# Joining float64 words with one shift-and-or in an attention and expert-layer kernel on one core

## The chip, the cores and the metric

The kernel runs on one core of a Trainium2 chip. The core has a matrix engine (TensorE, PE in the profile, its weight loads PEld), a vector engine (DVE), an activation engine (ACT), a general engine (POOL, nearly unused here) and a queue that issues DMAs (SP). Each engine runs its own list of instructions in order, and they wait for one another by semaphores. The metric is the device time of one execution in microseconds. Before the change its median over three runs is 596.85 us (596.62 to 597.36).

## The reference

Causal attention over 4 batches of 12 heads, 448 positions and 64 columns per head, then two matrix products with an ELU between them. The weights `moe_w_in` and `moe_w_out` are float64.

```python
def _attn_ref(q, k, v):
    scores = scale * np.matmul(q, k.transpose(0, 1, 3, 2))
    scores = np.where(mask, -1000000000.0, scores)
    scores = scores - np.max(scores, axis=-1, keepdims=True)
    attn = np.exp(scores)
    attn = attn / (np.sum(attn, axis=-1, keepdims=True) + 1e-09)
    return np.matmul(attn, v).astype(np.float32)

def _moe_ref(x, w_in, w_out):          # x: 1792 x 768, w_in: 768 x 2048, w_out: 2048 x 768
    h = x @ w_in
    g = np.where(h > 0.0, h, alpha * (np.exp(np.minimum(h, 0.0)) - 1.0))
    return (g @ w_out).astype(np.float32)
```

## The kernel before

**Attention.** Two heads share the 128 partitions. For each pair of heads PE forms the scores (sc, line 535), DVE adds the mask and takes the row minimum of the negated scores (line 440), ACT takes the exponential with the row sums (line 444), PE transposes (tr, line 566), a copy brings the transpose to SBUF (at, on ACT at line 570 or on DVE at line 571), and PE multiplies with the values (av, line 585). The six head pairs of batch 0 come first of all, two at a time (`first_two`); the other batches are spread between the matmuls of the expert layer.

**The expert layer.** A float32 product is done as three products of a high and a low part (hp and op, lines 786 to 788). The split into the parts is `hi_lo` (lines 741 to 748): the high part is a copy to a shorter type, on ACT (line 744) or DVE (line 745), the low part a subtraction on DVE (line 747). `in_two` (line 735) does that for a weight tile of 128 x 768 (whl), `split_row` (line 862) for a row of activations (ph, pl). For batches 2 and 3, and for the second product of all, seven products of combined blocks stand in place of eight (`mixed`, `mixed_h`, `mixed_o`), for which DVE adds and subtracts blocks.

**Float64 weights.** The chip gets each weight as two 32-bit words. `convert` (line 697) makes float32 of a tile of 16 x 768 columns (w_in, one for each of 16 blocks) or 512 columns (w_out, 24 tiles). It clamps the high word as a float (DVE, line 705), rescales it on ACT so that its exponent comes right (line 709), shifts the bits left by three (DVE, line 710), takes the top three bits of the low word (ACT, line 713) and adds them to the shifted word (DVE, line 716, a custom operation on halves of 16 bits in the profile). The result is split for the matmuls and stored to DRAM for later use.

**The order of work.** The kernel first writes all of its instructions as a list of works (`plan.add`), each with one or two ways to be done (an engine, a cost and a function), its buffers and a due time from the order of PE's matmuls. `draft` then goes through them like a scheduler: the engine that can start soonest takes, of the works that can start by then, that with the earliest wanted time. The wanted time is the due time less an entry of the table `SOONER`, by the number of the work; a positive entry draws the work forward. A work with two ways stays with the first (ACT) unless the second (DVE) would be done at least `LEAST` = 0.8 us sooner:

```python
                    if way:
                        if w.want > s + self.SOON:
                            continue
                        ...
                        if max(t, free.get(e0, 0.0)) + before + c0 < s + cost + self.LEAST:
                            continue
```

The order that comes out is the order of each engine's instruction list, SP's DMAs included.

Of the kernel before, what the change touches and what calls it, by code (L numbers as in the profile page):

```python
# [11 lines left out]
U32 = mybir.dt.uint32  # L12
# [96 lines left out]
class Plan:  # L109
# [21 lines left out]
    def add(self, ways, reads=(), writes=(), due=None, size=0.0, hold=(), after=None):  # L131
# [24 lines left out]
        return w  # L156

    SOONER = {
# [50 lines left out]
    }  # L209

    def rank(self):
# [17 lines left out]
    def draft(self, shift):  # L229
# [17 lines left out]
        while len(order) < len(self.works):  # L247
            starts = {}
            for w, t in ready.items():
# [19 lines left out]
                for way, (eng, cost, _, port) in enumerate(w.ways):  # L269
                    s = max(t, free.get(eng, 0.0))  # L270
                    if w.size and w.want > s + self.FAR:
                        s = max(s, moved - self.QUEUE)
                    if port:
                        s = max([s] + [f for e, f in ported.items() if e != eng])
                    if way:
                        if w.want > s + self.SOON:
                            continue
                        e0, c0 = w.ways[0][:2]
                        before = sum(
                            o.ways[0][1] for o, to in ready.items()  # L280
                            if to <= s and o.ways[0][0] == e0 and o.want < w.want and o is not w
                        )
                        if max(t, free.get(e0, 0.0)) + before + c0 < s + cost + self.LEAST:
                            continue
                    starts.setdefault(eng, []).append((s, w.want, w.n, way, w))
# [51 lines left out]
def attention_moe_kernel(ctx, tc, qk, v, w_in, w_out, out):  # L337
# [62 lines left out]
    def act(n, fn, more=0.05):  # L400
        return ("ACT", more + 0.84e-3 * n, fn, False)

    def dve(n, fn, rate=1.05e-3, more=0.067, port=False):
        return ("DVE", more + rate * n, fn, port)
# [294 lines left out]
    def convert(key):  # L699
# [7 lines left out]
        ), 0.55e-3, 0.06, True), [(r, 1)], [w])  # L707

        plan.add(act(size, lambda: nc.scalar.activation(wf(), wf(), AF.Prelu, scale=REBIAS, alpha=2.0 ** 32), 0.09), [], [w])  # L709
        plan.add(dve(size, lambda: nc.vector.tensor_scalar(  # L710
            wf().bitcast(U32), wf().bitcast(U32), 3, None, op0=ALU.logical_shift_left
        ), 0.55e-3, 0.06, True), [], [w])
        plan.add(act(size, lambda: nc.scalar.activation(
            low().bitcast(I32), low(), AF.Copy, scale=2.0 ** -29
        ), 0.16), [], [(r, 0)])
        plan.add(dve(size, lambda: nc.vector.tensor_tensor(  # L716
            out=wf().bitcast(I32), in0=wf().bitcast(I32), in1=low().bitcast(I32), op=ALU.add
        ), 1.05e-3, 0.07, port=True), [(r, 0)], [w])
        if key[0] == "i":
            done(r)  # L720
            home, src = kin[key[1]], wf
# [470 lines left out]
```

## Time and profile before

| what | us |
|---|---|
| median of three runs | 596.85 |
| profiled execution | 597.11 |
| its span, first to last instruction | 595.3 |
| PE busy (share of the span) | 585.1 (98%) |
| PEld busy | 518.4 (87%) |
| DVE busy | 516.5 (87%) |
| ACT busy | 434.9 (73%) |
| POOL busy | 1.5 (0%) |

The profile is of one execution. Busy time is the time in which an engine has at least one instruction running; matmuls overlap, so that a busy PE may still run slower than it can. A line such as L786 is a line of the kernel; the names are those of the program's tiles, written `out<-in`. "Idle before" is the time in which an engine had nothing to run just before a group of instructions, with the engine that ended it. The granted clock is the share of full speed that the chip gave to TensorE.

### The profile page before, as it was taken

Reading aid. Unit: us, or ns where it says so; the run is one execution under the profiler, and the core shown is the slowest. Engines: PE = TensorE matmul, PEld = TensorE weight load, DVE = VectorE, ACT = ScalarE, POOL = GpSimd, SP = SyncE. Lnnn points to the kernel's source line nnn. Section 1 sums busy time; section 2 is a strip of 40 time slices with the busy share of each in tenths; the row PEclk is TensorE's granted clock in tenths of the full one; section 3 lists DMA queues with packets and bytes.
Section 4 is the critical chain, followed back from the end, with each engine's and each line's share of the span. In section 5 each row is a group of like instructions: output and inputs, shape, how many; then the busy total and the mean of one; then the engine's idle time right before and its main releaser. Section 6 shows DMA issues by size and latency. Waiting matters only on the chain.

```text
span 595.3 us, 11387 instructions
## 1 busy us (share of the span) xinstructions
PE 585.1 (98%) x4010; PEld 518.4 (87%) x4010; DVE 516.5 (87%) x1236; ACT 434.9 (73%) x996; POOL 1.5 (0%) x12
## 2 busy tenths in 40 slices
PE   7999999999999999999999999999999999999998
PEld 4767798889899898898888988999999999999997
DVE  5798999998989989999998899869888999998532
ACT  6999999897988889988786593455555768575310
POOL 0000000000000000000000000000000000000000
PEclk9989999999999999999999999999999999999999
DMA  8987976488689999796556579987854115344112
GB/s 245 407 281 241 297 247 188 161 269 278 177 270 347 329 313 339 238 299 204 157 134 197 164 231 334 332 276 232 261 165 132 54 55 184 96 137 133 52 40 74
DMA packets 81976, 127.58 MB, mean 214 GB/s; under 512 B 9472, under 2 KB 58112, under 8 KB 81920
## 3 DMA queue, kind: packets, MB, share of 16 engines
q1 hardware_dynamic: 81920, 126.87, 67.1%
q8 instruction: 31, 0.51, 0.3%
q14 instruction: 25, 0.20, 0.1%
HBM read 94.63 MB, written 32.21 MB: 213 GB/s over the span
## 4 chain that ended last, share of the span: by engine, by line
PE 91%; ACT 5%; DVE 2%; DMA 0%; issue 0%; SPq 0%; DVEq 0%
PE op L786 12%; PE hp L786 12%; PE op L787 12%; PE op L788 11%; PE hp L788 11%; PE hp L787 11%; PE av L585 7%; PE sc L535 7%; PE tr L566 6%; ACT a L444 3%; PE hp L809 2%; ACT at L570 1%; ACT w L709 1%; DVE a L440 1%; DMA k<-in_qk 0%; DVE w L716 0%
## 5 line engine op out<-in xcount | busy, mean ns | idle before, releaser
L786 PE MATMUL op<-ph,whl 128*128 128x448 f32 (+1 forms) x338 | 125.7, 372 | 0.0
L787 PE MATMUL op<-pl,whl 128*128 128x448 f32 (+1 forms) x338 | 123.4, 365 | 0.1
L788 PE MATMUL op<-ph,whl 128*128 128x448 f32 (+1 forms) x338 | 123.3, 365 | 0.0
L744 ACT ACTIVATE whl<-w 128x768 fp32r<-128x768 f32 x101 | 83.9, 840 | 53.6 <-PE op L788 36.5
L444 ACT ACTIVATE a<-a,nm 112x336 f32<-112x336 f32 (+3 forms) x192 | 99.8, 529 | 25.2 <-DVE nm L440 24.8
L747 DVE TENSOR_TENSOR whl<-w,whl 128x768 fp32r<-128x768 f32 x111 | 104.4, 951 | 3.2 <-ACT whl L744 2.6
L440 DVE CUSTOM_DVE_ANT_0 a<-sc,mask 112x448 f32<-112x448 f32 (+3 forms) x192 | 76.0, 444 | 12.3 <-PE sc L535 12.3
L786 PE MATMUL hp<-xh,whl 128*128 128x448 f32 x180 | 69.9, 388 | 0.0
L786 PEld LDWEIGHTS op<-ph,whl 128*128 128x128 f32 x338 | 63.5, 188 | 6.5 <-issue 0.6
L787 PEld LDWEIGHTS op<-pl,whl 128*128 128x128 f32 x338 | 63.5, 188 | 5.3 <-DVE pl L747 0.5
L788 PEld LDWEIGHTS op<-ph,whl 128*128 128x128 f32 x338 | 63.5, 188 | 5.2
L788 PE MATMUL hp<-xh,whl 128*128 128x448 f32 x180 | 65.9, 366 | 1.1 <-DVE whl L747 1.1
L787 PE MATMUL hp<-xl,whl 128*128 128x448 f32 x180 | 65.8, 366 | 0.0
L787 PE MATMUL hp<-pl,whl 128*128 128x448 f32 x168 | 61.4, 365 | 0.0
L786 PE MATMUL hp<-ph,whl 128*128 128x448 f32 x168 | 61.4, 365 | 0.0
L788 PE MATMUL hp<-ph,whl 128*128 128x448 f32 x168 | 61.4, 365 | 0.0
L566 PEld LDWEIGHTS tr<-ident,a 112*112 112x112 f32 x480 | 49.4, 133 | 10.2 <-ACT a L444 2.8
L570 ACT ACTIVATE at<-tr 112x448 f32<-112x448 f32 x116 | 56.5, 542 | 2.1 <-PE tr L566 2.1
L566 PE MATMUL tr<-ident,a 112*112 112x112 f32 x480 | 56.4, 260 | 1.6 <-ACT a L444 1.0
L585 PEld LDWEIGHTS av<-at,v 112*64 112x64 f32 x960 | 47.3, 139 | 8.9 <-issue 3.7
L585 PE MATMUL av<-at,v 112*64 112x112 f32 x960 | 52.9, 265 | 0.5 <-ACT at L570 0.4
L882 ACT ACTIVATE m<-hp 128x448 f32<-128x448 f32 x56 | 29.9, 541 | 25.1 <-PE hp L788 15.7
(94 smaller groups left out, 951.4 us busy)
## 6 DMA issues: line engine op xcount, KB each, us to landing
w<-kin SPq DMA_DIRECT2D x41, 384.0 KB, 5.0
w<-in_w_in SPq DMA_DIRECT2D x16, 768.0 KB, 7.8
w<-in_w_out SPq DMA_DIRECT2D x24, 512.0 KB, 6.0
w<-sout SPq DMA_DIRECT2D x32, 384.0 KB, 3.6
w<-kout SPq DMA_DIRECT2D x24, 384.0 KB, 3.4
kin<-w SPq DMA_DIRECT2D x16, 384.0 KB, 6.0
sout<-w SPq DMA_DIRECT2D x12, 512.0 KB, 5.9
sin<-w SPq DMA_DIRECT2D x16, 384.0 KB, 4.4
```

What stands on the lines that cost most here:

```text
L440: plan.add(dve(n, lambda: nc.vector.tensor_tensor_reduce(out=a()[:, c], in0=sc()[:, c], in1=mask[:, S - n:], op0=ALU.add, op1=ALU.min, sca ...
L444: plan.add(act(n, lambda: nc.scalar.activation(a()[:, c], a()[:, c], AF.Exp, bias=nm()[:, x:x + 1], scale=-1.0, accum_out=su()[:, x:x + 1] ...
L535: nc.tensor.matmul(sc[half]()[:, lo:lo + n], q(d, x, i), k(d, y, n), start=j == 0, stop=j == len(split) - 1,)
L566: nc.tensor.transpose(tr()[:, chunk(x)], group["a"][half]()[:, chunk(x)], ident)
L570: act(w, lambda: nc.scalar.activation(at()[:, :w], tr()[:, :w], AF.Copy)),
L585: nc.tensor.matmul(av()[half_of(half), chunk(i)], u["v"]()[:, half, c], at()[:, chunk(x)], start=c == 0, stop=c == i,)
L744: act(n, lambda: nc.scalar.activation(h(), x(), AF.Copy), 0.09),
L747: sub = lambda eng: lambda: eng.tensor_tensor(out=l(), in0=x(), in1=f32(h()), op=ALU.subtract)
L786: nc.tensor.matmul(acc(), wh(k), xh(), start=first, stop=False, skip_group_check=more)
L787: nc.tensor.matmul(acc(), wh(k), xl(), start=False, stop=False, skip_group_check=more)
L788: nc.tensor.matmul(acc(), wl(k), xh(), start=False, stop=last, skip_group_check=more)
L882: plan.add(act(S, lambda: nc.scalar.activation(m(), h(), AF.Relu, scale=-1.0), 0.14), [h], [m])
```

## The change

Three things change. In `convert` the shift of the high part and the extraction of the low bits become two ways of one work: ACT takes the low bits with a scale and a bias that make it round down, or DVE shifts the high part. A single scalar_tensor_tensor on DVE then shifts the other word and joins the two with a bitwise or. The fixed shift and the integer addition go. The table `SOONER` is replaced by another (484 entries in place of 394). A new table `WAY` fixes the way of 70 works (0 is the first way, ACT; 1 is the second, DVE), and `draft` follows it without the comparison above.

```diff
     SOONER = {
-        12: -55.9, 54: -74.4, 55: -11.4, 87: -3.7, 88: 96.4, 91: -8.2, 93: -22.7, 105: 26.2, 131: -16.6,
...
+        12: -19.4, 27: 20.6, 28: 91.9, 34: 2.8, 43: 60.4, 44: -72.9, 54: 38.6, 55: 79.7, 67: -11.3, 73:
...
+    WAY = {
+        44: 0, 95: 1, 228: 1, 275: 1, 278: 0, 283: 1, 288: 1, 297: 1, 446: 1, 449: 0, 462: 1, 534: 0,
+        728: 0, 801: 1, 810: 1, 817: 1, 819: 1, 844: 0, 901: 1, 1006: 0, 1042: 1, 1066: 1, 1187: 1,
+        1216: 0, 1218: 1, 1304: 0, 1317: 0, 1342: 0, 1380: 1, 1382: 1, 1426: 1, 1667: 1, 1679: 1, 1693:
+        1, 1818: 1, 1822: 1, 1854: 1, 1867: 1, 1896: 0, 1930: 1, 1934: 1, 2000: 1, 2001: 1, 2056: 1,
+        2058: 1, 2106: 1, 2206: 1, 2262: 1, 2444: 0, 2455: 1, 2557: 1, 2591: 1, 2608: 1, 2621: 1, 2648:
+        1, 2685: 1, 2689: 1, 2710: 1, 2779: 1, 2804: 1, 2806: 0, 2846: 1, 2848: 1, 2850: 1, 2861: 1,
+        2876: 1, 2904: 1, 2908: 1, 2917: 1, 2979: 1,
     }
...
-                    if way:
+                    if self.WAY.get(w.n, way) != way:
+                        continue
+                    if way and w.n not in self.WAY:
                         if w.want > s + self.SOON:
                             continue
...
-        plan.add(dve(size, lambda: nc.vector.tensor_scalar(
-            wf().bitcast(U32), wf().bitcast(U32), 3, None, op0=ALU.logical_shift_left
-        ), 0.55e-3, 0.06, True), [], [w])
-        plan.add(act(size, lambda: nc.scalar.activation(
-            low().bitcast(I32), low(), AF.Copy, scale=2.0 ** -29
-        ), 0.16), [], [(r, 0)])
-        plan.add(dve(size, lambda: nc.vector.tensor_tensor(
-            out=wf().bitcast(I32), in0=wf().bitcast(I32), in1=low().bitcast(I32), op=ALU.add
-        ), 1.05e-3, 0.07, port=True), [(r, 0)], [w])
+        bits, shifted = (lambda: wf().bitcast(U32)), []
+        plan.add([
+            act(size, lambda: nc.scalar.activation(
+                low().bitcast(I32), low(), AF.Copy, scale=2.0 ** -29 * (1.0 - 2.0 ** -20), bias=-0.4999
+            ), 0.16),
+            dve(size, lambda: (shifted.append(1), nc.vector.tensor_scalar(
+                bits(), bits(), 3, None, op0=ALU.logical_shift_left
+            )), 0.55e-3, 0.06, True),
+        ], [(r, 0)], [(r, 0), w])
+
+        def join():
+            x, by, how, y = (low(), 29, ALU.logical_shift_right, bits()) if shifted else (bits(), 3, ALU.logical_shift_left, low())
+            nc.vector.scalar_tensor_tensor(out=bits(), in0=x, scalar=by, in1=y, op0=how, op1=ALU.bitwise_or)
+        plan.add(dve(size, join, 1.05e-3, 0.07, port=True), [(r, 0)], [w])
```

## Rows read from the trace of the kernel before

**Rows 1.** The page: share of the chain that ended last, by engine.
```profile
PE 91%; ACT 5%; DVE 2%; DMA 0%; issue 0%; SPq 0%; DVEq 0%
```

**Rows 2.** PE's waits; last row, its weight loads' from 10 to 46: us, times, longest.
```profile
PE hp L788 <- DVE whl L747: 1.1, 1, 1.1
PE tr L566 <- ACT a L444: 1.0, 1, 1.0
PE tr L566 <- DVE xf L609: 0.5, 1, 0.5
PE av L585 <- ACT at L570: 0.4, 1, 0.4
...
PEld av L585 <- DVE w L710: 1.3, 1, 1.3
```

**Rows 3.** DVE in order of time, 218 to 241: start us, us, instruction [idle before].
```profile
221.98 0.43 DVE L710 TENSOR_SCALAR w<-w 128x512 uint32<-128x512 uint32 x1 [0.86 <-ACT w L709]
...
234.44 0.95 DVE L747 TENSOR_TENSOR whl<-w,whl 128x768 fp32r<-128x768 f32 x1
```

**Rows 4.** Busy time by stretch: length, PE, PEld, DVE, ACT, POOL, granted clock, DMA.
```profile
15.00:31.00 16.00, 13.98 (x166) 10.86 (x164) 12.00 (x41) 16.00 (x49) 0.00 (x0) 1.00 1.03 402
31.90:35.30 3.40, 3.40 (x26) 2.09 (x28) 3.23 (x10) 3.27 (x13) 0.00 (x0) 0.51 1.04 289
60.00:210.00 150.00, 150.00 (x1193) 131.91 (x1191) 139.45 (x388) 135.75 (x331) 0.00 (x0) 1.00 0.81 258
210.00:240.00 30.00, 28.73 (x203) 25.22 (x200) 28.38 (x82) 27.48 (x70) 0.00 (x0) 1.00 0.98 325
480.00:540.00 60.00, 60.00 (x298) 55.60 (x297) 59.57 (x101) 41.77 (x76) 0.00 (x0) 1.00 0.38 115
```

**Rows 5.** PE in order of time, at 30 to 48 and 228 to 242 us.
```profile
30.56 1.25 PE L566 MATMUL tr<-ident,a 112*112 112x112 f32 x8 [1.02 <-ACT a L444]
...
33.35 3.09 PE L585 MATMUL av<-at,v 112*64 112x112 f32 x40
...
45.06 2.14 PE L585 MATMUL av<-at,v 112*64 112x112 f32 x40
...
235.46 0.47 PE L788 MATMUL hp<-xh,whl 128*128 128x448 f32 x1 [1.14 <-DVE whl L747]
```

**Rows 6.** Groups by line and shape, conversion: busy us, mean ns of one | idle before.
```profile
L713 ACT ACTIVATE w<-w 128x512 int32<-128x512 uint32 x24 | 16.1, 679 | 0.0
L716 DVE CUSTOM_DVE_ANT_0 w<-w,w 128x1536 uint16<-128x1536 uint16 x16 | 15.3, 955 | 0.5
L713 ACT ACTIVATE w<-w 128x768 int32<-128x768 uint32 x16 | 14.6, 948 | 0.0
L710 DVE TENSOR_SCALAR w<-w 128x512 uint32<-128x512 uint32 x24 | 10.2, 424 | 5.8 <-ACT w L709 5.6
L710 DVE TENSOR_SCALAR w<-w 128x768 uint32<-128x768 uint32 x16 | 8.9, 554 | 0.9 <-ACT w L709 0.9
```

**Rows 7.** Groups by line and shape: the nearest forms, and two-way works on DVE.
```profile
L747 DVE TENSOR_TENSOR whl<-w,whl 128x768 fp32r<-128x768 f32 x111 | 104.4, 951 | 3.2 <-ACT whl L744 2.6
L747 DVE TENSOR_TENSOR pl<-G,ph 128x448 fp32r<-128x448 f32 x64 | 37.8, 619 | 0.2
...
L745 DVE CAST whl<-w 128x768 fp32r<-128x768 f32 x10 | 5.6, 556 | 0.1
L884 DVE SCALAR_TENSOR_TENSOR u<-m,u 128x448 f32<-128x448 f32 x8 | 4.9, 618 | 0.1
L571 DVE COPY at<-tr 112x448 f32<-112x448 f32 x4 | 2.5, 621 | 0.8 <-PE tr L566 0.8
L745 DVE CAST ph<-s 128x448 fp32r<-128x448 f32 x2 | 0.8, 387 | 0.0
```

**Rows 8.** Chain that ended last, in order of time, 26 to 32: start us, us.
```profile
27.43 0.84 ACT w L713
28.27 0.85 ACT at L570 x2
```

More of the change, by code (lines that the diff above doesn't have):

```diff
@@ L158 @@
     SOONER = {
[50 rows of a table removed]
[61 rows of a table added]
+    }
+    WAY = {
[7 rows of a table added]
     }
```

109 rows, old and new, of the table SOONER are left out of this document.

## The prediction, made before the changed kernel ran

> **What bounds the kernel now.** The chain that ended last comes first. Of it, 91% is PE's, 5% ACT's and 2% DVE's [rows 1]. So an edit that touches only DVE and ACT can give no more than PE's lost time, wherever the cause of a loss is DVE or ACT. The list of PE's waits is the next view, since it says where that is. Beside the wait for the first load, which stays, it has four: 1.0, 0.5 and 0.4 us in the attention work at the start, and one of 1.1 us for a weight split by DVE (line 747), which DVE began at 234.44 us [rows 2, 3]. The table of stretches then shows how full each engine was where PE lost. From 15 to 31 us ACT is busy for all of its 16.00 us and PE for 13.98. In 210:240 PE has 28.73 of 30.00, DVE 28.38 and ACT 27.48. From 60 to 210 us, and from 480 to 540 us, PE is never idle, though DVE is nearly full (139.45 of 150, 59.57 of 60) [rows 4]. One loss more shows only in PE's granted clock: 0.51 from 31.9 to 35.3 us, so close to the lower of its levels (1.2 GHz of 2.4). Just before it PE had sat idle for 1.02 us until 30.56 us. The same 40 products of the values (av) took 3.09 us in that stretch and 2.14 us at 45 us [rows 4, 5]. So 0.95 us is lost on these alone, and at most 3.4 x 0.49 = 1.7 us in all; I take 1.5, since little else lies in the stretch and nearly all of it is PE's work.
>
> What DVE or ACT could give back is then about 1.1 us at 234, some 1.9 us of waits at the start (1.0 + 0.5 + 0.4), and 1.5 us of clock: 4.5 us, 0.8%. Nothing else is in reach of this change, unless tighter switching between kinds of matmuls brings some tenths.
>
> **The change, part by part.** *The conversion.* Before, each of 40 float64 tiles (16 of 768 columns, 24 of 512) costs five instructions: a clamp on DVE, a rescale on ACT, a shift on DVE (L710), the low bits on ACT (L713), and a join on DVE (L716). After, the shift and the low bits are alternatives, so each tile has four. If ACT takes the low bits, DVE loses the shift: 16 x 0.554 + 24 x 0.424 = 8.9 + 10.2 = 19.1 us, were it so for all 40. If DVE shifts, ACT loses the low bits: 16 x 0.948 + 24 x 0.679 = 15.2 + 16.3 = 31.5 us by duration, 30.7 us by busy time [rows 6]. Back to back, DVE's instructions overlap by about 0.1 us. Nothing of this is PE's, so the gain is only what reaches the places above.
>
> *The new join.* One scalar_tensor_tensor on 32-bit words replaces a custom operation on 16-bit halves, which takes 955 ns for 768 words. The form with two bitwise operations does not occur before. Nearest rows: a scalar_tensor_tensor with both inputs in SBUF (u<-m,u) takes 618 ns for 448 columns, and a tensor_tensor on the same size 619; a tensor_tensor on 768 takes 951 [rows 6, 7]. On the tensor_tensor's line, (951 - 619) / 320 = 1.04 ns per column and 154 ns on top, 512 words take 686 ns. I take 951 and 686: no change. Below, it could run like the one-input shift (554 and 424), which would save 16 x 0.40 + 24 x 0.27 = 12.8 us of DVE. Above, twice the slope gives 1.75 and 1.22 us, or 16 x 0.80 + 24 x 0.53 = 25.5 us more. The Trainium skill speaks for that upper end: "Vector Engine (DVE) Microarchitecture Reference", section "Points that are easy to get wrong", says that a scalar_tensor_tensor whose two sources lie in SBUF and are not bf16 runs at half throughput. The trace disagrees for floats with its 618 ns against 619; for words no row shows it.
>
> The low bits get a bias as an immediate and lose a rounding. An activation with a scale and no bias is in the trace already; I take the same 948 and 679 ns. The low bits or the shift now also wait for the rescale. On ACT that costs nothing where the rescale is ahead in its queue anyway. Behind a shift that waits stands the rest of DVE's queue, as behind L710 before. No DMA is added and none dropped; the store of a converted tile follows its join as before.
>
> *Which engine.* I counted the works in the order in which the code adds them, less one for each conversion already passed. All 70 numbers of the new table then fall on works with two ways. They are 18 weight splits (15 to DVE), 26 row splits (22 to DVE), 8 query/key splits (6), 9 copies of transposes (8), 7 conversions (4), one other copy (to DVE) and one other split. The rest go by the old rule, which leaves a work on ACT unless DVE is sooner by 0.8 us. DVE so gets at least 15 x 0.556 + 22 x 0.387 + 8 x 0.621 = 21.8 us, against 10 x 0.556 + 6 x 0.387 + 4 x 0.621 = 10.4 us of the same kinds before [rows 7]: 11.4 us more. With some 30 conversions left to ACT it loses 30/40 x 19.1 = 14.3 us. So DVE's total falls by about 3 us (by 8 if ACT takes the low bits of all 40, and it rises by 11 if of none). The larger relief is ACT's: 10/40 x 31.5 = 8 us of low bits, and the moved splits and copies besides.
>
> *At 234 us.* PE waits for the split that DVE began at 234.44 us. In the 13 us ahead of it DVE ran three shifts of 0.43 us, the first at 221.98 us [rows 3]. Without them the split comes up to 1.29 us sooner, less what the first shift's own wait for ACT (0.86 us) keeps. The stall is 1.14 us [rows 5]. I take -1.1 (bounds 0, if these tiles are shifted by DVE, and -1.3, which is PE's whole idle time in 210:240 [rows 4]).
>
> *At the start.* In the chain of waits ACT stands without a break there. One low-bits extraction (0.84 us) stands in it ahead of the exponentials for which PE waits until 30.56 us [rows 5, 8]. DVE shifts that tile anyway, so on DVE's side it is free. One copy of a transpose that the table gives to DVE takes another 0.43 us (two take 0.85) from ACT [rows 8]. Together -1.27, of which PE can use up to the 1.02 us that it waited. I take -0.9 (bounds 0 and -1.9, all three waits). If the cover goes, that is if DVE, which has 4 of 16 us free there [rows 4], runs late with the copy, the 0.62 us [rows 7] is PE's wait.
>
> *Behind it.* The weight loads of the products that begin at 33.35 us (on the row of PE's loads) wait 1.3 us on DVE, in a queue that a shift (L710) holds up [rows 2, 5]. Without the shift, 0.554 us less the overlap, -0.45 (bounds 0 and -1.3).
>
> *The clock and the order.* The fall to 0.51 stays in my sum: PE still has waits ahead of it. The table of moved works is new throughout (394 entries before, 484 after), and its effect on PE I take as 0, with bounds from the small waits: -1 to +2.8 (below).
>
> Sum: -1.1 - 0.9 - 0.45 = -2.45 us. The profiled execution took 597.11 us, which is 1.8 us around its span of 595.3, and stands 0.26 us over the median of 596.85. From the median: 594.4 us.
>
> **The rivals.** *The clock does not fall at the start.* With the waits of 0.5 and 1.0 us gone, PE may stay at 2.4 GHz: -1.5 more, 592.9 us. For it: the fall comes right behind such a wait. Against: ACT is full from 15 to 31 us, and PE can lack work there without such a wait.
>
> *No change.* PE had only one wait behind 31 us; the new order brings one or two like it elsewhere (1.1 us each) and eats the gains: 596.3 us. For it: DVE and ACT are still both over 90% in 60:210 [rows 4], so any work that is late meets a queue.
>
> *Slower: the works fixed on DVE in 480:540.* By their due times eight of these are there: three weight splits and five row splits, 3 x 0.556 + 5 x 0.387 = 3.6 us, against the two row splits on DVE before (ph<-s, 0.8 us) [rows 7]. DVE has 0.43 us free in 60 [rows 4], so it falls back by 2.4 us by 540. PE pays as soon as its lead over DVE is less than that. Against: PE never waited in that stretch, and behind 540 us DVE waits for PE. Price: 2.4 us with none of the start's gains and half of the gain at 234: 596.85 + 2.4 - 0.55 = 598.7 us.
>
> *The join at half speed.* DVE then has 25.5 us more and 14.3 less, or +11.2, nearly all between 31 and 260 us, where it has 10.55 us free in 60:210. Some 4 us reach PE: 600.9 us. It is the mechanism that the page's rule gives, and the floats' row speaks against it.
>
> **How the numbers follow.** Forecast 0.40 (594.4), clock stays up 0.20 (592.9), no change 0.22 (596.3), slower by DVE 0.14 (598.7), join at half speed 0.04. What can be told from no change is 0.2%, 1.2 us: 595.65 to 598.05. The forecast ends within that in one of ten cases, and the slower case in two of its 0.14. Faster 0.36 + 0.20 + 0.03 = 0.59, slower 0.12 + 0.04 = 0.16, the same 0.25. The range runs from 592.0 (below the clock's case, with the tenths of switching) to 598.2 (half of the slower case is out). The forecast's own range is 593 to 595.7.
>
> **What would show it.** L710 and L713 together have 40 instructions, about 30 of them on ACT, and the join near 951 and 686 ns. PE's wait at 234 us is gone. ACT has no low bits ahead of the exponentials near 30 us. PE has no new wait from DVE in 480:540. A join over 1.2 us, a PE wait of over 1 us in any other place, or a second stretch at half clock would make the forecast wrong.

## The result and the profile after

After: 601.68 us median (600.16 to 603.04), before in the same runs 596.99 (596.62 to 597.36); ratio 1.007, interval 1.005 to 1.0091. The change makes the kernel 0.7% slower (0.5 to 0.9); the forecast was 594.4 us and faster. The profiled execution took 602.23 us, 5.1 us more than the one before; its span is 600.4 against 595.3.

The chain that ended last, share of the span by engine (page of after):
```profile
PE 71%; DMA 11%; DVE 11%; ACT 4%; issue 2%; SPq 1%; DVEq 0%; ACTq 0%
```
Before, PE had 91% and transfers 0% [rows 1]. Transfers now stand in the chain for 11% of the span, so the first place to look is not an instruction but what DVE and ACT wait for.

PE's waits of the whole span, after: us, times, longest.
```profile
PE sc L558 <- DMA k<-in_qk: 4.1, 1, 4.1
PE av L608 <- DVE xf L490: 0.8, 1, 0.8
PE av L608 <- ACT at L593: 0.7, 2, 0.4
PE tr L589 <- ACT a L467: 0.7, 2, 0.5
PE sc L558 <- DVE nm L463: 0.7, 1, 0.7
PE sc L558 <- ACT at L593: 0.5, 1, 0.5
PE op L815 <- DVE pl L775: 0.4, 2, 0.2
PE hp L814 <- DVE whl L773: 0.4, 1, 0.4
PE hp L816 <- DVE whl L775: 0.3, 1, 0.3
PE hp L814 <- ACT at L593: 0.2, 1, 0.2
```
The single wait of 1.1 us at 234 us [rows 2] is gone; beside the first load there are nine kinds of small ones, 4.7 us in all against 3.0 before. The 1.7 us more don't add up to the 5 us that were lost. Busy time by stretch, after (length, PE, PEld, DVE, ACT, POOL, granted clock, DMA share, GB/s):
```profile
31.90:35.30 3.40, 3.40 (x50) 2.44 (x48) 3.40 (x9) 3.40 (x13) 0.00 (x0) 1.00 1.02 349
234.20:237.60 3.40, 3.40 (x11) 2.58 (x12) 3.33 (x14) 3.35 (x11) 0.00 (x0) 0.50 1.06 331
180.00:210.00 30.00, 29.59 (x235) 25.79 (x234) 25.07 (x70) 26.50 (x62) 0.00 (x0) 1.00 0.96 322
210.00:240.00 30.00, 28.06 (x181) 23.64 (x181) 26.66 (x81) 24.00 (x62) 0.00 (x0) 0.94 1.03 320
240.00:270.00 30.00, 29.93 (x234) 26.31 (x233) 29.66 (x76) 25.47 (x59) 0.00 (x0) 1.00 0.87 274
480.00:540.00 60.00, 60.00 (x298) 55.60 (x297) 58.73 (x103) 37.19 (x69) 0.00 (x0) 1.00 0.38 112
```
PE loses in 180:240, where before it lost only the split's wait [rows 4]; DVE is busy for less of that time than it was (26.66 us in 210:240 against 28.38). Behind it DVE is full, but it was so before the change too:
```profile
240.00:270.00 30.00, 30.00 (x239) 27.09 (x239) 29.86 (x74) 26.59 (x61) 0.00 (x0) 1.00 0.87 259
```
In this profile the stretch at half clock lies at 234.2 us in place of 31.9: it follows two stops of PE (0.50 us until 231.62, 0.66 until 234.09), as the one before followed one of 1.02 us [rows 5].

The conversion's groups, after: busy us, mean ns of one | idle before.
```profile
L745 DVE SCALAR_TENSOR_TENSOR w<-w,w 128x512 uint32<-128x512 uint32 x24 | 16.5, 688 | 3.0 <-ACT w L735 2.7
L745 DVE SCALAR_TENSOR_TENSOR w<-w,w 128x768 uint32<-128x768 uint32 x16 | 15.3, 956 | 1.6 <-ACT w L735 1.5
L735 ACT ACTIVATE w<-w 128x512 int32<-128x512 uint32 x22 | 14.7, 667 | 0.0
L735 ACT ACTIVATE w<-w 128x768 int32<-128x768 uint32 x11 | 10.2, 931 | 0.0
L738 DVE TENSOR_SCALAR w<-w 128x768 uint32<-128x768 uint32 x5 | 2.8, 560 | 1.0 <-ACT w L732 1.0
L738 DVE TENSOR_SCALAR w<-w 128x512 uint32<-128x512 uint32 x2 | 0.8, 420 | 0.0
```
33 of 40 tiles take their low bits from ACT, and the join costs what the forecast took, 956 and 688 ns (951 and 686).

To see PE's loss where "busy" hides it, I worked out for each stretch its length less the matmuls that started in it at their steady price (0.2025 us for 448 columns of split weights, 0.225 for the scores, 0.096 for a transpose, 0.052 for a product of the values). All stops, slow clock and switching between kinds of matmuls are in it; missing records blur it by some tenths. The scores have several shapes, so the level of a column moves by up to some us with the prices taken; the differences between the rows don't, beyond some tenths. "Again" is a second profile of the changed kernel, and e1 to e17 are the experiments:
```
PE's lost us         0:60  60:180  180:240  240:330   sum to 330
before               13.4    4.1     3.7      2.8       24.0
after                12.5    4.2     8.2      4.5       29.4
after, again (e16)   13.2    5.0     5.8      5.5       29.6
e1  old order        13.2    4.3     2.9      2.7       23.2
e2  new order        13.3    4.2     7.8      7.1       32.4
e4  half loads       14.0    4.3     2.0      5.3       25.5
e5  sums on POOL     14.7    4.4     3.8      5.3       28.2
e8  more traffic     13.4    4.1     3.5      3.0       24.0
e9  five later       12.5    5.0     6.0      5.1       28.6
e12 nine places      14.1    5.4     3.8      5.3       28.6
e13 casts on ACT     14.4    4.1     3.9      5.6       28.0
e15 both             12.7    4.9     3.6      5.7       26.9
e17 all three        13.2    4.6     2.0      5.7       25.5
```
All of the 5 us is lost before 330 us. In the first profile of the changed kernel 4.5 us of it lie in 180:240 and 1.7 in 240:330; in the second 2.1 and 2.7, and 0.9 in 60:180. The sums of the two agree, but in one column they differ by up to 2.4 us, so a smaller difference between two single profiles in one column says little.

### The profile page after: what moved, and what is told of

It reads as the page before. It is cut to its first block, busy times and chain, and to the rows that moved or that the text cites. A ratio compares the mean times of both kernels' runs of the same rounds, so it can differ in the third digit from the quotient of the medians.

```text
span 600.4 us, 11313 instructions
## 1 busy us (share of the span) xinstructions
PE 588.6 (98%) x4010; PEld 519.9 (87%) x4010; DVE 517.9 (86%) x1240; ACT 409.4 (68%) x952; POOL 1.5 (0%) x12
## 4 chain that ended last, share of the span: by engine, by line
PE 71%; DMA 11%; DVE 11%; ACT 4%; issue 2%; SPq 1%; DVEq 0%; ACTq 0%
PE op L814 10%; PE op L815 10%; PE op L816 10%; PE hp L814 9%; PE hp L815 9%; PE hp L816 9%; PE av L608 5%; PE tr L589 4%; PE sc L558 4%; DMA w<-kin 3%; DMA kout<-w 2%; DVE whl L775 2%; DMA rdram<-tt 2%; DVE a L463 2%; ACT a L467 2%
## 5 line engine op out<-in xcount | busy, mean ns | idle before, releaser
L467 ACT ACTIVATE a<-a,nm 112x448 f32<-112x448 f32 (+3 forms) x192 | 99.9, 527 | 34.0 <-DVE nm L463 33.4
L772 ACT ACTIVATE whl<-w 128x768 fp32r<-128x768 f32 x92 | 76.6, 840 | 39.9 <-PE op L816 20.0
L593 ACT ACTIVATE at<-tr 112x448 f32<-112x448 f32 x110 | 53.8, 541 | 6.5 <-PE tr L589 6.4
```

What stands on the lines that cost most here:

```text
L467: plan.add(act(n, lambda: nc.scalar.activation(a()[:, c], a()[:, c], AF.Exp, bias=nm()[:, x:x + 1], scale=-1.0, accum_out=su()[:, x:x + 1] ...
L593: act(w, lambda: nc.scalar.activation(at()[:, :w], tr()[:, :w], AF.Copy)),
L772: act(n, lambda: nc.scalar.activation(h(), x(), AF.Copy), 0.09),
```

## The experiments

**Instructions or order: e1, e2.** e1 keeps the order of before, with the shift emitting nothing, and takes the new low bits and join for all 40 tiles; e2 keeps the new order and gives the 33 tiles of ACT's way the old shift and an add:
```diff
-    wf().bitcast(U32), wf().bitcast(U32), 3, None, op0=ALU.logical_shift_left      # e1: lambda: None
-    low().bitcast(I32), low(), AF.Copy, scale=2.0 ** -29
+    low().bitcast(I32), low(), AF.Copy, scale=2.0 ** -29 * (1 - 2.0 ** -20), bias=-0.4999
+    scalar_tensor_tensor(out=wf, in0=wf, scalar=3, in1=low(), op0=shift_left, op1=bitwise_or)
 # e2, in join(), where ACT took the low bits:
+    tensor_scalar(bits(), bits(), 3, None, op0=shift_left); tensor_tensor(out=wf, in0=wf, in1=low(), op=add)
```


> The kernel before, its order of work unchanged, with the new instructions: no shift, the low bits rounded down on ACT for all 40 tiles, the shift-and-or as the join. Theory 'order' (the loss of 4.7 us lies in the new order of work): 595.0 to 597.0 us, the wait of 1.1 us at 234 us shorter or gone. Rival 'instructions' (the new join or the low bits with a bias hold up DVE or ACT): 599 us or more, with a join over 1 us or a new wait behind it.

> The changed kernel, its order and its ways unchanged, but where ACT takes the low bits (33 tiles) the old shift and integer addition stand in place of the one join: some 14 us more on DVE. Theory 'order': at least as slow as the changed kernel, 602 to 607 us, since DVE is full from 240 to 330 us and gets more. Rival 'instructions': back towards 597 to 599 us.


e1: 596.2 us, ratio 0.9979 (0.997 to 0.9988). e2: 605.8 us, 1.0153 (1.0135 to 1.0171). So the new instructions gain 0.2% in the old order, and the new order loses: 601.68 - 596.2 = 5.5 us lie between two kernels with the same new kinds of instructions. "New order" stands here for both new tables, and they do more than reorder: after has more on DVE than e1 (517.9 us busy against 501.3) and less on ACT (409.4 against 435.4). What the order costs and what the choice of engines costs was not tried apart, but for 13 casts in e13. Much the same relief of DVE (a busy time of 501.3 us in e1 against 516.5, of 517.9 in after against 531.3 in e2) is worth 1 us in the old order and some 4 us in the new. PE's wait at 234 us in e1, and two of its stretches:
```profile
PE hp L786 <- DVE whl L745: 0.6, 1, 0.6
```
```profile
30.90:34.30 3.40, 3.40 (x16) 1.52 (x15) 2.64 (x6) 3.40 (x12) 0.00 (x0) 0.50 1.07 253
210.00:240.00 30.00, 29.36 (x211) 26.12 (x208) 26.82 (x79) 27.59 (x71) 0.00 (x0) 1.00 1.03 344
```
The shifts gone, that wait is 0.6 us in place of 1.1; the fall of the clock stays. e1 is faster than both kernels.

**Transfers: e3, e4.** Each tile of w_out loads half of its words (256 KB in place of 512) and reads them twice, so that it is another matrix; e3 in the kernel before, e4 in the changed one:
```diff
-    out = r()[:, :4] ; src = w_out[..., 2 * x:2 * x + 2]
+    out = r()[:, 4:6] ; src = w_out[..., 2 * x:2 * x + 1]      # read with to_broadcast
```


> The kernel before; each of the 24 loads of w_out words brings only half of its words (256 of 512 KB), which are read twice, so the output is not the reference's. Order and instruction counts unchanged. 6.3 MB less to move, 4.7 MB of it before 200 us. Theory 'transfers' (DMA is the limit from 150 to 240 us, and the new order arrives there 2 MB behind): little changes here, 595 to 597 us. Rival 'engines' (the new order makes DVE or ACT late, whatever the transfers do): the same 595 to 597 us; the pair with the next run decides.

> The changed kernel with the same halved loads of w_out words (the output is not the reference's). Theory 'transfers': the lag of 180 to 240 us goes, 596 to 598 us, within 1.5 us of the kernel before with halved loads. Rival 'engines': 3.5 us or more above it, 599 to 601 us.


e4: 598.31 us, ratio 1.0017 (1.0005 to 1.003), 3.4 us less than after. e3: 600.65 us, 1.0072 (1.0048 to 1.0095): a relief that makes the kernel before slower, which neither theory had expected. In e4 PE never stops in 180:240:
```profile
180.00:210.00 30.00, 30.00 (x248) 26.71 (x247) 25.82 (x72) 26.28 (x60) 0.00 (x0) 1.00 0.89 281
210.00:240.00 30.00, 30.00 (x208) 26.82 (x209) 28.67 (x84) 27.36 (x70) 0.00 (x0) 1.00 0.94 284
```
Halving the loads so has a price of its own in the old order, and the 3.4 us of e4 are what is left of its gain if it has one in the new order too. In e3 SP's queue stood 7.6 us behind the landing of the softmax sums in 55:100 (3.6 before), and DVE 3.2 us behind a store near 200 us. How the halved loads bring this about was not tried.

**SP's queue: e5, e6.** In after SP stands 12.5 us in 88:160 behind stores of the softmax sums that wait for DVE. The sums' transfers go to GpSimd's queue, e5 in after, e6 in before:
```diff
-    nc.sync.dma_start(out=home, in_=turned()) ... nc.sync.dma_start(out=r()...)
+    nc.gpsimd.dma_start(out=home, in_=turned()) ... nc.gpsimd.dma_start(out=r()...)
```


> The changed kernel, same order and ways, but the small transfers of the softmax sums (the store rdram<-tt and the two loads R<-rdram of each block) are issued from GpSimd's queue, which is idle, in place of SP's. SP's queue then no longer stands 12.5 us in 88:160 behind stores that wait for DVE's transpose. Theory 'held queue' (the loads of w_out's words come late because SP stands behind these stores; the 2 MB that are late at 150 us make the DMA full in 180:240): the rate in 90:150 rises from 186 to over 205 GB/s, PE's waits in 180:240 shrink, and the time falls from 601.7 to 597.5-599.5 us. Rival 'order itself' (the loads are late because the new order lists them late or because their slots come free late): the time stays at 601-602.5 us and the loads start at the same times within 2 us.

> The kernel before with the same move of the sums' transfers from SP's to GpSimd's queue: the control. SP's queue stood 3.9 us in 88:160 behind these stores, and 3.6 us in 55:100 behind their landing. Held queue: 596-597.2 us (little to win, PE never waits there). Rival: the same, 596.5-597.5. If the move itself costs (GpSimd's issue, later sums), both kernels get slower alike, and it is read from this run: over 598 would say so.


e5: 604.0 us, 1.0098 (1.007 to 1.0127). e6: 602.85 us, 1.0071 (1.0038 to 1.0103). The move costs 4 to 5 us in the control, so e5 doesn't tell what the held queue costs. It tells something else: the loads of w_out came no earlier (w_out's second load at 114.8 us; 112.2 in after, 101.0 before), and still PE's loss in 180:240 is 3.8 us, below both profiles of after. That SP stands behind these stores is not what makes the loads late.

**Late loads, more traffic: e7, e8**, both in the order of before. e7 issues five early loads of w_out 2 to 9 places later in SP's queue; e8 adds eight copies of 256 KB in DRAM (kout holds the converted tiles of w_out there):
```diff
+    late = {1: 3, 2: 2, 3: 8, 4: 9, 6: 9}          # e7: load number: places
+    nc.gpsimd.dma_start(out=spare, in_=home)       # e8: behind each of the first 8 stores of kout
```


> The kernel before, all engines' orders kept, but five of the first seven loads of w_out's words (those that SP issued at 101, 108, 117, 119 and 135 us) are issued 2 to 9 places later in SP's queue, about when the changed kernel issued its own. Theory 'transfers' (late loads leave more to move in 150:240, where the DMA is full, and PE waits there): 1.5-4 us slower, 598.5-601 us, with PE's new waits between 180 and 250 us and a lower rate in 90:150. Rival 'engines' (what PE loses in 180:240 comes from how the works lie on DVE and ACT, not from loads): within 0.6 us of the kernel before, 596.4-597.8.

> The kernel before, plus eight copies in DRAM of 256 KB each (2 MB; the first eight converted tiles of w_out, each copied behind its store from GpSimd's idle queue, between about 120 and 190 us); nothing waits for them. Theory 'transfers': the 2 MB push the transfers of 180:240 back, as the 2 MB that the changed kernel has open at 150 us do: 599-602.5 us, with PE's new waits in 180:250. Rival 'engines': the DMA has room enough (0.72 of it busy in 150:180), and the time stays at 596.4-597.8 us.


e7: 605.22 us, 1.0124 (1.0095 to 1.0153). e8: 597.89 us, 1.0004 (0.9989 to 1.0018). ACT's first wait in 100:175 and PE's longest behind the first load, both e7:
```profile
ACT w L727 <- DMA w<-in_w_out: 10.6, 4, 5.3
```
```profile
PE av L598 <- ACT at L583: 3.5, 1, 3.5
```
And e8 in the stretches that were to suffer:
```profile
180.00:210.00 30.00, 30.00 (x235) 26.59 (x235) 28.03 (x75) 25.21 (x58) 0.00 (x0) 1.00 1.03 338
210.00:240.00 30.00, 28.73 (x204) 25.23 (x201) 28.65 (x83) 27.88 (x70) 0.00 (x0) 1.00 1.03 341
```
The amount of traffic is not the cause: 2 MB more leave PE's 28.73 us as they were [rows 4], at a DMA share of 1.03. Late loads can be one: an engine runs its instructions in order, so ACT stood 10.6 us at low bits whose words had not landed, and PE stood 3.5 us for a copy of a transpose behind them. But e7 lost at 135 to 165 us, not in 180:240 as I had expected of it, so it doesn't show that these loads are what the new order pays for.

**Conversions later: e9, e10, e11.** In after DVE stood 3.5 us for words (165 to 174 us) and 2.0 us for a place (one of the eight buffers that weight tiles share) that a store of kout still held, and ACT 2.0 us for two converted tiles fetched back (kin). These are their waits on transfers in 160:245, and below them all of DVE's waits in the same stretch before; ACT had none on a transfer there either:
```profile
DVE w L728 <- DMA w<-in_w_out: 3.5, 3, 1.9
DVE w L728 <- DMA kout<-w: 2.0, 1, 2.0
ACT whl L772 <- DMA w<-kin: 2.0, 2, 1.0
```
```profile
DVE w L710 <- ACT w L709: 4.0, 6, 1.6
DVE at L571 <- PE tr L566: 0.8, 1, 0.8
DVE G L884 <- ACT m L883: 0.3, 1, 0.3
```
The store as a piece of the chain of waits, the clamp it releases, and where the chain returns to PE:
```profile
219.21 6.92 DMA kout<-w
226.15 0.44 DVE w L728
...
292.15 0.55 DVE pl L775
292.70 0.04 issue
292.74 0.47 PE op L815
```
From 164.9 to 292.7 us this chain holds no matmul (in e16 from 206.1 to 293.0); before, only 219.9 to 239.3 us were such a stretch. e9 puts the five conversions that stood up to 3 us later in all engines' orders, e10 18 of 24 by 2.5 us, e11 the same in before:
```diff
+    LATE = {("o", 0, 1): 3.0, ("o", 3, 1): 3.0, ("o", 1, 1): 3.0, ("o", 3, 3): 3.0, ("o", 4, 3): 3.0}
+    if wait: held.append((s + wait, w, fn))        # emitted once the plan's time has passed
```


> The changed kernel; five conversions of w_out (the three whose clamps stood 3.5 us on DVE behind their loads at 165-174 us, and the two whose slot DVE awaited for 2.0 us at 224) are put up to 3 us later in the order of all engines, with everything else as it was. Theory 'standing in line' (DVE and ACT run their instructions in order; the new order puts conversions right where the plan expects their loads, the transfers land later, and what stands behind them reaches PE): DVE's waits on transfers in 160:245 fall from 5.5 us to under 2, PE loses less in 180:240, and the time falls from 601.7 to 598.5-600.5 us. Rival 'too much on DVE' (DVE is late by the works that the table fixes on it; its waits are harmless idle time): 601-602.5 us, and later conversions may even cost.

> The same for 18 of the 24 conversions of w_out (all but the first six tiles), each some 2.5 us later. Standing in line: also the waits of DVE and ACT behind conversions between 180 and 226 us (ACT behind the clamp 0.3 to 4.1 us, DVE behind the low bits) shrink: 598-600.5 us. If stores that come later hold SP's queue and that outweighs it: up to 603. Rival: 601-603 us.

> The control: the kernel before with the same 18 conversions some 2.5 us later. There DVE and ACT never stood behind a transfer between 100 and 245 us, so standing in line expects no gain: 596.5-598.5 us, a little slower if anything. If later conversions were good in themselves (less in the queues ahead of the splits that PE waits for), this kernel would gain too: under 596.


e9: 602.07 us, 1.0073 (1.0048 to 1.0097). e10: 611.53 us, 1.0212 (1.018 to 1.0245). e11: 609.56 us, 1.0199 (1.0179 to 1.022). In e9 the waits of DVE and ACT on transfers in 160:245 fell from 7.5 us to 3.3, DVE's to 2.5 and not under 2, and the time is that of after. Conversions that come 2.5 us later cost the kernels 10 and 12 us, so being put later has a price of its own, which can hide a gain in e9. "Standing in line" forecast the wrong time three times; e9 to e11 neither show it nor rule it out.

**Places, DVE behind 240 us: e12 to e17.** e12 (and e14 in before) has nine places for weight tiles and one place less for rows of activations; e13 runs the 13 high parts that the plan puts on DVE in 235:330 on ACT; e15 is both; e16 is the changed kernel again; e17 is e15 with e4's halved loads:
```diff
-    bufs = SHARED.get(slot) or PLACES[slot]
+    bufs = (SHARED.get(slot) or PLACES[slot]) + (slot == "w") - (slot == "row")          # e12, e14, e15, e17
-    dve(n, lambda: nc.vector.tensor_copy(h(), x()), ...)
+    dve(n, lambda: nc.scalar.activation(h(), x(), AF.Copy) if 235 < plan.now < 330 else ...)  # e13, e15, e17
```


> The changed kernel in its own order, with nine places for the weight tiles w in place of eight (and 70 in place of 71 for the row tiles, which pays for the room). A load or a clamp into w then waits for a place that was let go one tile earlier: in 179-226 us the chain of waits ran four times through such a place (w<-kin 8.14, kout<-w 5.85, w<-kin 8.43, kout<-w 6.92 us). Theory 'places' (the new order lets too few weight tiles be on their way while transfers take 6 to 8 us): DVE no longer waits 2.0 us for a store of kout, the loads w<-kin start earlier, PE loses 2-4 us less in 180:240, and the time is 598-600 us. Rival 'DVE late behind 240' (what counts is that DVE is full from 240 to 330 us, and all that was lost before only shows there): 601-602.5.

> The changed kernel in its own order; the high parts of weight and row splits that stand on DVE between about 235 and 330 us (5 of 768 columns, 8 of 448, 5.9 us; 1.3 us before the change) run on ACT, at the same place in the order. DVE has 29.66, 29.76 and 29.09 of 30 us there, ACT 25.47, 23.18 and 16.18. Theory 'DVE late behind 240': DVE gets 5 us free, PE loses 1-2.5 us less in 240:330, 599.5-600.8 us. Rival 'places' (the loss comes from transfers before 240): no more than 0.5 us, 601-602.2 us.

> The control: the kernel before with nine places for w and 70 for rows. PE's only loss behind 60 us there was 1.1 us for a split at 234 us, behind DVE and no transfer: 596.8-597.8 us by both theories; over 598 would say that the lost row place costs.

> The changed kernel in its own order with both edits: nine places for w (70 for rows) and the 13 high parts of 235-330 us on ACT. From about 205 to 291 us the chain of waits of the changed kernel goes through DVE, with one step in it (kout<-w, 6.9 us) in which DVE waits for a place of w. Theory 'a line through DVE' (that stretch is bound by DVE: what the place gives back is taken again by DVE's full queue behind it, and the other way round): both edits together give more than the sum of each (1.3 and 0 us), 598-599.5 us, and the chain goes back to PE before 280 us. Rival 'the places alone': 600-601 us, as with the nine places.

> The changed kernel itself, once more: a second profile, to tell what of its losses belongs to the kernel and what to one execution. If the line through DVE binds, PE's waits before 240 us lie elsewhere in this profile, but its time agrees within 0.3% (600-603 us) and DVE is full again in 240:300. If the losses of 180:240 come from fixed places in the order, the same waits stand at the same times.

> The changed kernel in its own order with three reliefs at once: loads of w_out's words halved (half of its words is read twice, so the output is that of other weights), nine places for w, and the 13 high parts of 235-330 us on ACT. Alone these gave 3.4, 1.3 and 0 us. In every profile of the new order the chain of waits goes through DVE up to 291 us, and PE loses 4.5 to 5.7 us in 240:330 (2.8 in the kernel before). Theory 'a line through DVE and the transfers': with all of it relieved PE's loss in 240:330 falls to 3.5 or less and the time to 595.5-597.5 us. Rival 'PE's own order' (the new order of the products itself, its switching, costs the rest there): the loss in 240:330 stays at 4.5-5.7 and the time at 597.8-599 us, as with the half loads alone.


e12: 600.33 us, 1.0048 (1.0031 to 1.0065). e13: 601.82, 1.0076 (1.0061 to 1.0091). e14: 597.26, 1.0002 (0.999 to 1.0014). e15: 600.16, 1.0052 (1.0037 to 1.0068). e16: 601.58, 1.008 (1.0065 to 1.0095). e17: 598.11, 1.0011 (1.0 to 1.0023). Stretches of e12, of e13, and of after for the last of them:
```profile
210.00:240.00 30.00, 30.00 (x239) 26.70 (x236) 28.60 (x84) 26.22 (x65) 0.00 (x0) 1.00 1.03 323
```
```profile
240.00:270.00 30.00, 29.47 (x225) 25.17 (x224) 28.14 (x71) 26.14 (x61) 0.00 (x0) 1.00 0.82 254
300.00:330.00 30.00, 30.00 (x239) 26.63 (x238) 25.55 (x66) 21.76 (x53) 0.00 (x0) 1.00 0.48 143
```
```profile
300.00:330.00 30.00, 30.00 (x243) 26.52 (x242) 29.09 (x74) 16.18 (x45) 0.00 (x0) 1.00 0.44 127
```
With a ninth place PE has no stop left in 210:240, and the time is about 1.3 us lower (the intervals overlap, so this size is loose). In e13 DVE has 1.5 and 3.5 us more free in these two stretches, and nothing comes of it: PE's loss in 240:330 is 5.6 us. The two together give what the place gives alone. e17 has all reliefs and is where the halved loads alone were; its 5.7 us in 240:330 say that neither the transfers, nor the places, nor these 13 casts make that part.

Most of it is seen in the loads of PE's weights, which that first list of PE's waits leaves out. One such stop in after, weight load and product:
```profile
290.46 0.19 PEld L815 LDWEIGHTS op<-pl,whl 128*128 128x128 f32 x1 [0.50 <-DVE pl L775]
290.47 0.47 PE L815 MATMUL op<-pl,whl 128*128 128x448 f32 x1 [0.22 <-DVE pl L775]
```
The waits of the weight loads on DVE in 240:330, after and then e17:
```profile
PEld op L815 <- DVE pl L775: 1.4, 3, 0.6
PEld op L816 <- DVE whl L775: 0.3, 1, 0.3
```
```profile
PEld op L825 <- DVE pl L785: 1.0, 3, 0.5
PEld op L826 <- DVE whl L785: 0.9, 2, 0.7
```
Before and in e1 there is none. The low parts that DVE makes (pl, whl) hold them up by 1.7 to 2.3 us in the profiles of the new order, and by 4.6 us in e2, whose DVE has more to do. The rival of e17, that the new order changes more often between kinds of matmuls, has the traces against it: PE changes kind 47 times in 240:330 before, 41 times after and 39 times in e17. Why the low parts come late stays open: DVE was as full before (87.07 us of the 90, 88.51 after), and the 13 casts taken from it in e13 leave 2.0 us of these waits.

e16 also answers for 180:240. DVE's waits on words and on the place are there again (3.6 and 2.2 us), and so are PE's two longest stops (until 231.90 and 234.36 us, in the first profile until 231.62 and 234.09): they belong to the order and not to one execution. e16 has no fall of the clock (its mean is 1.0); the stretch of the first profile's fall, in e16:
```profile
234.20:237.60 3.40, 3.24 (x19) 2.75 (x20) 3.33 (x14) 3.40 (x10) 0.00 (x0) 1.00 1.01 263
```
This execution took no less time than the first profile's (602.6 and 602.23 us), so the fall is not the price.

## Why the prediction was wrong

*The conversion* was right: 33 of 40 low bits on ACT (forecast about 30), join 956 and 688 ns. The Trainium skill, "Vector Engine (DVE) Microarchitecture Reference", section "Points that are easy to get wrong", says that a scalar_tensor_tensor whose two sources lie in SBUF and are not bf16 runs at half throughput. The prediction took that as half of a tensor_tensor's rate, and by this reading the trace disagrees: 956 ns is the time of a tensor_tensor of that size (951) [rows 7], and the rival of the half-speed join is out. Read against an instruction with one input, the sentence agrees with the trace: per column the join takes (956 - 688) / 256 = 1.05 ns, the shift (554 - 424) / 256 = 0.51 [rows 6].

*Which engine*: DVE's sum was to fall by about 3 us and rose by 1.4 (516.5 to 517.9), within the bounds; ACT lost 25.5 us. *480:540*: PE has no wait there (60.00 of 60, DVE 58.73), as forecast; the rival of a slower kernel named this stretch, and it was the wrong one.

*At 234 us* (-1.1): the wait is gone in after, but with the whole order. In the old order, e1, without any of the shifts, it shrank by 0.5 us: the term was twice too large.

*At the start and behind it* (-0.9, -0.45): to 60 us PE lost 13.4 us before, 12.5 and 13.2 in the two profiles after, and 14.4 in e13, which is the same kernel that far. The spread is wider than the 1.35 us, so whether they came can't be told. ACT still had a low-bits extraction among the exponentials, though near 30 us, which the prediction had ruled out. *The clock*: the fall was kept in the sum, and where it lies changes from one execution to the next: in after at 234 us, in e16 nowhere, in e13 at the start:
```profile
28.00:30.00 2.00, 2.00 (x18) 1.72 (x17) 1.87 (x7) 2.00 (x7) 0.00 (x0) 0.50 1.00 412
```

*The failed step* is the one sentence on the table: "its effect on PE I take as 0, with bounds from the small waits: -1 to +2.8". The new tables measure +5.5 us (e1 to after), twice the upper bound. I took the order as something that can add a few waits like those before, and the signs of being wrong were chosen to match: a new wait of over 1 us. None came; PE's longest new wait is 0.8 us, and the loss is many small ones. The order of before had slack in its transfers: DVE and ACT never stood behind one between 100 and 245 us. In the new one three clamps, a place and two fetches stand behind transfers, and PE loses in 180:240. The rows that I read, engines' busy times, could not show that slack; the trace of before has it in the waits of DVE and ACT on transfers, which I did not list.

Shown is that the tables cost it and not the new instructions (e1, e2), that halving the loads takes 3.4 us back, and that a ninth place takes about 1.3 of the same. Ruled out as the cause by itself are the amount of traffic (e8) and the high parts on DVE behind 240 us (e13); e9 leaves the five conversions that stood open. In 240:330 the new order loses 1.7 to 2.9 us more than the old one (e2 left out), of which PE's weight loads wait 1.7 to 2.3 us for DVE's low parts. Why these come late is open, and so is how much of the 5.5 us is the order and how much the choice of engines. Undoing the tables piece by piece was not tried.

## What to carry to other kernels

An order that is fitted to one program is brittle: of seven edits that moved, lightened or added something in the order of before (e1, e3, e6, e7, e8, e11, e14), four cost 3 to 12 us, and one gained 1. When a change comes with a new order, forecast the instructions and the order apart, and bound the order by what such moves cost rather than by the waits that are there now; and test the instructions in the old order first, which here is the better kernel (e1, 596.2 us). Before that, list the waits of the engines beside the bottleneck on transfers: where there are none, there is a slack that a new order can spend. Such a wait is a sign and not a price: between 100 and 245 us DVE and ACT stood 1.7 us behind transfers in e1 and 3.4 us in e8, and neither kernel is slower than before. A list of PE's waits needs that of its weight loads beside it.

## What the runs showed of the hardware

2 MB more of copies in DRAM, at a DMA share of up to 1.03, changed nothing in the time (e8, 341 GB/s against 325 in 210:240). Moving the small transfers of the softmax sums from SP's to GpSimd's queue cost 4 to 5 us (e6: 602.85 us against 597.55, ratio 1.0071), though GpSimd had next to nothing else to do (1.5 us busy before). A stretch at half clock comes and goes between executions of one kernel (at 234 us in one profile of the changed kernel, nowhere in the next), and one of them has no price that could be told. Executions of the kernel before with a mean granted clock of 1.0 have a median of 597.4 us (45 of them), those with 0.996 or 0.997 one of 597.3 (30), but those with 0.994 one of 598.7 (8).
